# Making the gate product of a fused attention and expert kernel from half-precision parts that a DMA transposes, with the planner's table of numbers chosen anew

## The chip, the cores and the metric

The kernel runs on one core of one Trainium2 chip. The metric is device time in microseconds (us), the median of three runs. The engines are TensorE (PE in the profile, with its weight loads as PEld), VectorE (DVE), ScalarE (ACT), GpSimd (POOL), and SyncE (SP), which issues nearly all DMAs.

## The reference, cut to what matters

Three stages follow each other on 1536 tokens of width 512 (2 sequences of 768 tokens, 8 heads of 64):

```python
x   = attention(q, k, v)                 # causal window of 128, 4 sink positions
h   = x @ w_in                           # 512 -> 2048
g   = (a0 + a1*h + a2*h**2 + a3*h**3) / (1 + |b0|*|h| + |b1|*h**2 + 1e-6)
y   = g @ w_out                          # 2048 -> 512
logits = y @ w_gate                      # 8 experts
e   = argmax(logits);  p = softmax(logits)[e]
out = p * (relu(y @ w1[e]) @ w2[e])      # first `capacity` tokens of each expert, else 0
```

The kernel uses (g @ w_out) @ w_gate = g @ (w_out @ w_gate). The small matrix w_out @ w_gate, 2048 x 8, called `wgo`, gives every token's logits without its y. It is the "gate product" of this study.

## The kernel before, in words

**Work.** Attention is done in 24 halves (12 blocks of 128 tokens, two groups of heads each). The product x @ w_in with its rational function is done in 24 units (6 chunks of 256 tokens, 4 column groups of w_in); a unit is four blocks of 12 matmuls (`unit_mm`, L828), so there are 96 blocks. Float32 weights are held as the sum of two float16 tiles, a high part and a low part, and a product is three float16 passes. `conv` splits the 16 pieces of w_in and then of w_out: a load of 512 KB to a staging slot `st`, three integer operations on DVE (L315, L325, L329), the high part on ACT (L337), the low part on POOL, DVE, or ACT with PE, by a letter of the strings CI and CO (G: POOL; S: POOL; V: DVE; P and R: two opening matmuls L285, a subtracting matmul L279, ACT).

**The gate product.** `wg_group(f)` runs after each of the 16 pieces of w_out (`conv_wout` calls it). Before the change it transposes the piece on PE (L878: four 128 x 128 parts, high and low, against a float16 identity `id16`, summed in a PSUM bank), copies the bank to a float32 tile `wt` on ACT (L882), multiplies it by the float32 `wgate` on PE (L890, four column groups), copies 128 x 128 out on ACT (L892), sums the four groups on PE against a selector `gsel` (L897), and copies 128 x 8 to `wgo` on DVE (L900). `wg_split` makes the float16 parts of `wgo` for each quarter.

**What follows from it.** `first_logits` (L1092) needs all of wgo, the first tokens' g and its split; then `route` and `pick` choose the first expert on the chip, whose weights are then loaded over the tiles of w_out (`load_expert`), while PE makes y (`ffn_y`, L1110 and L1130), the expert's hidden layer and the outputs (`outp`, L1154). The units of the later chunks are worked off in between, until the end.

**What sets the order.** Every job is a Python generator that names, before each step, the engine, an assumed duration and the slots that it takes (`yield PE(0.45, "b", "wt")`). The class `Plan` walks through the jobs, gives each engine the ready step that can start first, with ties by a key, and writes the instructions in that order. Engines run their own instructions in order. The keys, letters and slot counts come from the table PRM; PRM is what "the order" means here. Where PE would stand idle by the planner's reckoning in the first part of the program, the planner writes filler matmuls of 256 columns (`idle`, L491). A step on SP counts as done `lat` plus 2.1 us after its issue:

```python
AFTER = {"PE": 0.2, "ACT": 0.17, "DVE": 0.16, "POOL": 0.12, "SP": 2.1}
```

The slots that matter: `b` (PSUM banks), `st` (2 staging tiles), `wf` (512-column scratch tiles), `wt` (1).

Of the kernel before, what the change touches and what calls it, by code (L numbers as in the profile page):

```python
# [19 lines left out]
P = 128  # L20
# [15 lines left out]
CH = 256  # L36
NCH = NT // CH
NU = 4 * NCH
PRM = dict(LA=11.205, RATE=1.224, LC=6.29, LO=5.079, BATCH=1, T0=-15.603, dS=1.502, TW=50.81, dW=6.982,
           T1=-24.174, d1=6.704, T2=67.865, d2=5.437, CI='PSPPSGGGGGGGVPPG', CO='GGGSVGPRVSSSSGGG',  # L40
           RE='PPPPPSSPPPSPPSSSPPPPPPPP', CC='G', LL=3, rb=5, gp=5, GS='GVVGGGGV', VE=1, rr=13.375, rs=42.651,
           rt=-30.248, LD=-7.643, TF=150, FG=0.033, NE=6, eps=0, WT=-60.91, NB=4, VS1=14, BK=-26.717, dK=13.517,
           dO=0.808, eb=2, SE='G', st=2, wf=2, rc=1, xt=2, ab=2, qb=2)


class Plan:
# [147 lines left out]
def SP(dur, *take, lat=0.0):  # L194
    return "SP", dur, take, lat, None, None
# [10 lines left out]
def _build(ctx, tc, nc, io, ns, window, cap):  # L206
# [21 lines left out]
    def wf_(k):  # L228
        return stg.tile([P, 512], I32, name=f"wf{k}")
# [13 lines left out]
    def bank(k):  # L243
        return (bps[0] if k < R["NB"] else bps[1]).tile([P, 512], F32, name=f"b{k}")
# [8 lines left out]
            plan.give(slot, tok)  # L253

    for name, n in (("st", R["st"]), ("wf", R["wf"]), ("g", R["gp"]), ("rb", R["rb"]), ("rc", R["rc"]), ("xt", R["xt"]),
                    ("e", R["eb"]), ("a", R["ab"]), ("mx", 4), ("q", R["qb"]), ("k", 3), ("v", 3), ("wt", 1), ("sc", 1),
                    ("b", R["NB"])):
        plan.slot(name, range(n))

# [1 line left out]
    ident = cst.tile([P, P], F32, name="ident")  # L261
    lmask = cst.tile([P, 4, P], U8, name="lmask")
    ones16 = cst.tile([P, P], F16, name="ones16")
    id16 = cst.tile([P, P], F16, name="id16")
    n16 = [cst.tile([P, P], F16, name=f"n16{j}") for j in range(2)]
    tri16 = cst.tile([P, P], F16, name="tri16")
    gsel = cst.tile([P, E], F32, name="gsel")
# [186 lines left out]
    qp = pool(att, "qp", 1)  # L454
    ahp = pool(att, "ahp", 1)
    kp = pool(att, "kp", 1)
    wgt = pool(att, "wgt", 1)
    ps_s = None if dense else pool(ctx, "ps_s", 1, space=PSUM)
    vs = [kp.tile([96, DM], F16, name=f"vs{b}") for b in range(B)] if ns else None
    smask = [kp.tile([P, 4, ns], F32, name=f"smk{i}") for i in range(2)] if ns else None  # L460
# [408 lines left out]
    def wg_group(f):  # L869

        yield ("wait", "wgate")
        yield ("wait", "c3")
        yield PE(0.45, "b", "wt", cols=512)
        kb = plan.got("b")
        tp = bank(kb)
        for d in range(KD):
            for j in range(2):
                T.matmul(out=tp[:, d * P:(d + 1) * P], lhsT=w_out[j][:, f, d * P:(d + 1) * P], rhs=id16,  # L878
                         start=(j == 0), stop=(j == 1))
        yield ACT(0.478)  # L880
        wt = wgt.tile([P, KD, P], F32, name="wt")
        A.activation(out=wt, in_=tp.rearrange("p (d f) -> p d f", d=KD), func=AF.Copy, scale=2.0 ** -8)  # L882
        plan.give("b", kb)
        yield PE(0.36, "b", cols=166)
        kb = plan.got("b")
        wp = bank(kb)

        wg = wgate.rearrange("p k e -> p (k e)")
        for d in range(KD):
            T.matmul(out=wp[32 * d:32 * d + 32, 0:P], lhsT=wg, rhs=wt[:, d, :], start=True, stop=True)  # L890
        yield ACT(0.16)
        A.activation(out=wt[:, 0, :], in_=wp[:, 0:P], func=AF.Copy)  # L892
        plan.give("b", kb)
        yield PE(0.14, "b", cols=40)
        kb = plan.got("b")
        wp = bank(kb)
        T.matmul(out=wp[:, 0:E], lhsT=wt[:, 0, :], rhs=gsel, start=True, stop=True)  # L897
        plan.give("wt", 0)
        yield DVE(0.07)
        V.tensor_copy(out=wgo[:, f, :], in_=wp[:, 0:E])  # L900
        plan.give("b", kb)
# [449 lines left out]
    def gate_weights():  # L1351
        yield SP(0.6)
        SY.dma_start(out=wgate, in_=io["wg"].rearrange("(k p) e -> p k e", p=P))

    def identities16():
        yield ("wait", "ident")
        yield ACT(0.5)
        A.activation(out=n16[0], in_=ident, func=AF.Copy, scale=-2.0 ** -8)
        A.activation(out=n16[1], in_=ident, func=AF.Copy, scale=-2.0 ** 8)
        A.activation(out=id16, in_=ident, func=AF.Copy)  # L1360

    def constants3():
        yield ("wait", "ident")
# [258 lines left out]
```

## Time and profile before

| | |
|---|---|
| median of 3 runs | 343.35 us (342.74 to 344.38) |
| the profiled execution's own time | 343.65 us |
| its span, first to last instruction | 342.0 us |
| PE busy | 322.9 us (94%) |
| DVE busy | 263.5 us (77%) |
| ACT busy | 243.8 us (71%) |
| POOL busy | 196.3 us (57%) |
| mean granted TensorE clock | 0.989 |

A busy share is a mean over stages with different limits. Matmuls are pipelined, so the "mean ns" of one matmul is a latency; what it takes of PE is read from the starts of two blocks that follow each other. The profiled execution stands 0.3 us above the median of the runs.

### The profile page before, as it was taken

The numbers are of one execution on the slowest core, as the hardware profiler recorded it, in microseconds if no ns is written. First come the engines' busy times: TensorE is split into PE (matmuls) and PEld (weight loads), VectorE is DVE, ScalarE is ACT, GpSimd is POOL, SyncE is SP. The second block draws the span as 40 slices with busy tenths as digits, with TensorE's granted clock in tenths as the row PEclk, the third lists the DMA queues.
The fourth block names the chain that finished last, engine by engine and source line by source line (L and its number), as shares of the span: only waits on it lengthen the run. The fifth ranks groups of instructions, "written<-read, shape, count | busy, mean of one in ns | idle before, by whom it ended". The sixth has DMA issues, their size and how long they took to land.

```text
span 342.0 us, 9047 instructions
## 1 busy us (share of the span) xinstructions
PE 322.9 (94%) x3605; PEld 240.1 (70%) x3605; DVE 263.5 (77%) x509; ACT 243.8 (71%) x604; POOL 196.3 (57%) x209
## 2 busy tenths in 40 slices
PE   7999999988999999999999987999999999999990
PEld 5657787666786888788878876566667678777540
DVE  5988799999999987999997887740028898786641
ACT  2798889989989999899998954351038567586610
POOL 5467869496798658798998773310040054466400
PEclk9999999999999999999999998999999999999997
DMA  7755854846366490045211200300002431000001
GB/s 227 255 188 186 246 191 136 272 143 195 126 214 217 138 357 35 2 164 178 73 39 50 94 2 2 124 2 0 2 0 72 173 127 63 0 2 0 33 32 39
DMA packets 15336, 37.59 MB, mean 110 GB/s; under 512 B 2424, under 2 KB 2424, under 8 KB 15288
## 3 DMA queue, kind: packets, MB, share of 16 engines
q1 hardware_dynamic: 15288, 36.96, 32.4%
q8 instruction: 30, 0.49, 0.6%
q14 instruction: 18, 0.15, 0.1%
HBM read 30.66 MB, written 6.29 MB: 108 GB/s over the span
## 4 chain that ended last, share of the span: by engine, by line
PE 70%; ACT 12%; DVE 11%; DMA 3%; issue 2%; SPq 0%; POOL 0%; ACTq 0%; DVEq 0%
PE b L828 25%; PE b L1110 9%; PE b L1154 5%; PE b L491 4%; PE b L1130 4%; PE b L766 4%; PE sc L650 4%; PE b L926 3%; PE b L708 2%; ACT e L680 2%; PE b L1092 2%; ACT g L834 2%; PE b L878 2%; DMA st<-w_in 1%; DVE b L325 1%
## 5 line engine op out<-in xcount | busy, mean ns | idle before, releaser
L828 PE MATMUL b<-xt,win 128*128 128x256 f16 x1152 | 138.1, 273 | 1.6 <-POOL win L355 0.6
L828 PEld LDWEIGHTS <-win 128*128 128x128 f16 x1152 | 110.6, 99 | 22.5 <-issue 8.1
L853 POOL TENSOR_TENSOR rb<-rb,rc 128x1024 f32<-128x1024 f32 x24 | 58.7, 2446 | 1.0
L850 POOL TENSOR_SCALAR rc<-rb,cof 128x1024 f32<-128x1024 f32 x24 | 30.0, 1251 | 39.7 <-ACT rb L832 39.5
L700 POOL TENSOR_TENSOR e<-e,rs 128x512 f32<-128x512 f32 x24 | 25.3, 1052 | 38.7 <-DVE rs L687 20.6
L832 ACT ACTIVATE rb<-b 128x512 f32<-128x512 f32 x48 | 29.2, 608 | 19.0 <-PE b L828 18.6
L836 DVE TENSOR_TENSOR g<-g,b 128x512 f32<-128x512 f32 x48 | 32.7, 682 | 11.5 <-ACT g L834 11.3
L834 ACT ACTIVATE g<-b,cof 128x512 f32<-128x512 f32 x48 | 37.7, 785 | 0.0
L838 DVE SCALAR_TENSOR_TENSOR g<-g,cof,b 128x512 f32<-128x512 f32 x48 | 35.7, 743 | 0.8
L680 ACT ACTIVATE e<-sc,nm 128x132 f32<-128x132 f32 x84 | 31.5, 375 | 1.9
L1110 PE MATMUL b<-gs,wout 128*128 128x384 f16 x192 | 32.5, 326 | 0.0
L735 POOL TENSOR_SCALAR_AFFINE_SELECT upp<-low 128x512 f32<-128x512 f32 x20 | 14.1, 706 | 30.7 <-ACT low L729 30.7
L856 ACT ACTIVATE rb<-rb 128x1024 f32<-128x1024 f32 x24 | 25.4, 1057 | 7.6 <-POOL rb L853 7.6
L1110 PEld LDWEIGHTS <-wout 128*128 128x128 f16 x192 | 18.5, 99 | 13.1 <-issue 1.6
L1432 DVE SCALAR_TENSOR_TENSOR g<-g,cof,b 128x512 f32<-128x512 f32 x36 | 26.0, 743 | 1.2 <-ACT b L1420 0.9
L491 PE MATMUL b<-const-bfloat16-1.0 128*1 128x256 bf16 x162 | 23.2, 283 | 2.9 <-PEq L1611 0.9
L1420 ACT ACTIVATE b<-rb 128x512 f32<-128x512 f32 x36 | 21.4, 610 | 1.5 <-DVE wgo L900 1.4
L650 PE MATMUL sc<-kt,qt 64*64 64x128 f32 (+4 forms) x672 | 19.8, 249 | 0.9 <-DMA kt<-k 0.9
L650 PEld LDWEIGHTS sc<-kt,qt 64*64 64x64 f32 x672 | 17.0, 132 | 4.8 <-issue 2.3
L491 PEld LDWEIGHTS <-const-bfloat16-1.0 128*1 128x1 bf16 x162 | 12.4, 86 | 11.2 <-issue 6.2
L1114 DVE SCALAR_TENSOR_TENSOR gse<-b,gse 128x384 f16<-128x384 f32 x4 | 2.2, 558 | 22.5 <-ACT gse L1112 22.5
L766 PE MATMUL b<-low,v 128*64 128x128 f32 x192 | 18.9, 279 | 0.0
(187 smaller groups left out, 649.6 us busy)
## 6 DMA issues: line engine op xcount, KB each, us to landing
st<-w_in SPq DMA_DIRECT2D x16, 512.0 KB, 4.2
st<-w_out SPq DMA_DIRECT2D x16, 512.0 KB, 3.4
st<-w SPq DMA_DIRECT2D x8, 512.0 KB, 3.8
kt<-k SPq DMA_DIRECT2D x12, 264.0 KB, 4.1
qt<-q SPq DMA_DIRECT2D x12, 256.0 KB, 3.9
v<-v SPq DMA_DIRECT2D x12, 256.0 KB, 3.0
xs<-xt SPq DMA_DIRECT2D x12, 256.0 KB, 4.2
out<-wf SPq DMA_DIRECT2D x12, 256.0 KB, 4.3
```

The costliest lines, as they stand in the source:

```text
L491: T.matmul(out=fp[0:1, 0:256], lhsT=one[:, 0:1], rhs=one, start=True, stop=True)
L650: T.matmul(out=out, lhsT=q[:, t], rhs=kk[:, a:z], start=True, stop=True)
L680: A.activation(out=e[:, h, :], in_=wv[:, h, :], func=AF.Exp, scale=0.125, bias=nm[:, h:h + 1], accum_out=su[:, h:h + 1])
L766: T.matmul(out=o[r, c], lhsT=v_t[jobs[j][1]][:, hd], rhs=jobs[j][0][:, 2 * par + c, :], start=st, stop=sp, skip_group_check=c > 0)
L828: T.matmul(out=out, lhsT=l, rhs=r, start=(j == 0), stop=(j == len(jobs) - 1))
L832: A.activation(out=bb, in_=hp, func=AF.Abs, scale=2.0 ** -16)
L834: A.activation(out=g, in_=hp, func=AF.Identity, scale=cof[:, 3:4], bias=cof[:, 2:3])
L836: V.tensor_tensor(out=g, in0=g, in1=hp, op=ALU.mult)
L838: V.scalar_tensor_tensor(out=g, in0=g, scalar=cof[:, 1:2], in1=hp, op0=ALU.add, op1=ALU.mult)
L850: (G if eng == "G" else V).tensor_scalar(out=cc, in0=bb, scalar1=cof[:, 5:6], scalar2=cof[:, 4:5], op0=ALU.mult, op1=ALU.add)
L853: G.tensor_tensor(out=bb, in0=bb, in1=cc, op=ALU.mult)
L1110: T.matmul(out=yp[:, :n], lhsT=l, rhs=r, start=(j == 0), stop=(j == len(jobs) - 1))
```

## The change

The piece of w_out is no longer transposed on PE. SP issues two DMA transposes for each piece (L877 of the changed kernel), from the high and the low tile of w_out to one `wf` scratch tile, 128 x 512 float16 each. `wgate` is split once into two float16 tiles `gate16`. The product is three float16 passes over four column groups, 12 matmuls (L885). The copy of the transposed piece on ACT and the slot `wt` are gone, and `id16` is made only in the part of the program that runs when tokens are left over.

```diff
-        yield PE(0.45, "b", "wt", cols=512)
-        kb = plan.got("b")
-        tp = bank(kb)
-        for d in range(KD):
-            for j in range(2):
-                T.matmul(out=tp[:, d * P:(d + 1) * P], lhsT=w_out[j][:, f, d * P:(d + 1) * P], rhs=id16,
-                         start=(j == 0), stop=(j == 1))
-        yield ACT(0.478)
-        wt = wgt.tile([P, KD, P], F32, name="wt")
-        A.activation(out=wt, in_=tp.rearrange("p (d f) -> p d f", d=KD), func=AF.Copy, scale=2.0 ** -8)
-        plan.give("b", kb)
-        yield PE(0.36, "b", cols=166)
+        yield SP(1.2, "wf", lat=1.2)
+        kw = plan.got("wf")
+        w = wf_(kw)
+        wt = [w.bitcast(F16)[:, j * 512:(j + 1) * 512].rearrange("p (d f) -> p d f", d=KD) for j in range(2)]
+        for j in range(2):
+            SY.dma_start(out=wt[j], in_=w_out[j][:, f, :], transpose=True)
+        yield PE(0.3, "b", cols=400)
         kb = plan.got("b")
         wp = bank(kb)
-        wg = wgate.rearrange("p k e -> p (k e)")
-        for d in range(KD):
-            T.matmul(out=wp[32 * d:32 * d + 32, 0:P], lhsT=wg, rhs=wt[:, d, :], start=True, stop=True)
+        g = [t.rearrange("p k e -> p (k e)") for t in gate16]
+        for j, (a, b_) in enumerate(((g[0], wt[0]), (g[0], wt[1]), (g[1], wt[0]))):
+            for d in range(KD):
+                T.matmul(out=wp[32 * d:32 * d + 32, 0:P], lhsT=a, rhs=b_[:, d, :], start=(j == 0), stop=(j == 2))
         yield ACT(0.16)
-        A.activation(out=wt[:, 0, :], in_=wp[:, 0:P], func=AF.Copy)
+        wq = w.bitcast(F32)[:, 0:P]
+        A.activation(out=wq, in_=wp[:, 0:P], func=AF.Copy, scale=2.0 ** -16)
...
+        yield ACT(0.1)
+        A.activation(out=gate16[0], in_=wgate, func=AF.Copy, scale=256.0)
+        yield DVL(0.1)
+        V.scalar_tensor_tensor(out=gate16[1], in0=wgate, scalar=256.0, in1=gate16[0], op0=ALU.mult, op1=ALU.subtract)
```

In PRM nearly every key is another number. The letters that change: two pieces of w_out go from G to P (CO ends in GPP, before GGG), four splits of g that DVE made are made by POOL (GS is all G), some units' reciprocals change their path (RE), there are three `wf` slots in place of two, and the conversions of w_out get keys that lie closer together:

```diff
-PRM = dict(LA=11.205, RATE=1.224, LC=6.29, LO=5.079, BATCH=1, T0=-15.603, dS=1.502, TW=50.81, dW=6.982,
+PRM = dict(LA=11.877, RATE=1.2, LC=6.882, LO=2.195, BATCH=1, T0=-13.679, dS=1.29, TW=53.523, dW=7.072,
...
-           dO=0.808, eb=2, SE='G', st=2, wf=2, rc=1, xt=2, ab=2, qb=2)
+           dO=0.252, eb=2, SE='G', st=2, wf=3, rc=1, xt=2, ab=2, qb=2)
```

First place, PE around one gate product, the program before. Tiles carry a number that rises in the order in which the planner wrote the program; `b_` is a PSUM bank, `xt` the transposed x, `win` a part of w_in. The transposing matmuls stand four times as shown.

```order
L828 MATMUL b_1827<-xt_896,win_97 128x256
L878 LDWEIGHTS wout_98
L878 MATMUL b_1849<-id_87,wout_98 128x128
L878 LDWEIGHTS wout_99
L878 MATMUL b_1849<-id_87,wout_99 128x128
...
L828 MATMUL b_1827<-xt_897,win_96 128x256
...
L890 MATMUL b_1881<-wt,wgate 32x128 x4
```

The same place after the change. The product reads `wf_1806`, the scratch tile that the second pair of DMA transposes fills; between the writing of that tile and its reading PE has a filler, four transposes with their fifth (L707, L711) and one block of 12 (L827, bank 1883).

```order
L827 MATMUL b_1730<-xt_895,win_98 128x256
L490 MATMUL b_1866<-const-bfloat16-1.0 1x256
L707 MATMUL b_1868<-ident,e_1746 128x128 x4
L711 MATMUL b_1873<-ident,es_128 96x128
L827 MATMUL b_1883<-xt_895,win_97 128x256
...
L885 LDWEIGHTS gate_95
L885 MATMUL b_1905<-wf_1806,gate_95 32x128
...
L893 MATMUL b_1941<-gsel,wf_1806 128x8
```

The eight transposing matmuls are gone from PE, the four float32 products (L890) have become twelve float16 ones (L885), and what PE waits for is a DMA where it was a copy on ACT.

Second place, SP's queue where the loads of w_out begin, before (`st` is a staging tile, `qt`, `kt`, `v` a block of the attention's inputs):

```order
L295 DMA st_1549<-w_out 128x1024
L597 DMA v_1595<-v 128x512
L295 DMA st_1629<-w_out 128x1024
L295 DMA st_1708<-w_out 128x1024
L295 DMA st_1791<-w_out 128x1024
L586 DMA qt_1843<-q 128x512
```

And after:

```order
L295 DMA st_1595<-w_out 128x1024
L596 DMA v_1627<-v 128x512
L295 DMA st_1643<-w_out 128x1024
L877 DMA_TRANSPOSE wf_1701<-wout_99 128x4x128
L877 DMA_TRANSPOSE wf_1701<-wout_100 128x4x128
L295 DMA st_1728<-w_out 128x1024
L877 DMA_TRANSPOSE wf_1806<-wout_99 128x4x128
L877 DMA_TRANSPOSE wf_1806<-wout_100 128x4x128
L295 DMA st_1842<-w_out 128x1024
```

Each pair of transposes stands between loads of the next pieces, and a pair waits in SP's queue until the low part of its piece is written. Over the whole order the filler matmuls go from 162 to 201; of the 39 more, nearly all stand between the 11th and the 16th of the 96 blocks of `unit_mm`.

## Rows read from the trace of the kernel before

**Rows 1.** The page: span, and busy time, share and instructions of each engine.

```profile
span 342.0 us, 9047 instructions
PE 322.9 (94%) x3605; PEld 240.1 (70%) x3605; DVE 263.5 (77%) x509; ACT 243.8 (71%) x604; POOL 196.3 (57%) x209
```

**Rows 2.** Busy time by stretch: length, then each engine, granted clock, DMA share, GB/s.

```profile
60.00:84.00 24.00, 20.50 (x261) 14.97 (x258) 23.34 (x43) 21.85 (x61) 16.62 (x16) 1.00 0.64 210
84.00:110.00 26.00, 24.70 (x305) 20.23 (x305) 25.72 (x49) 23.95 (x60) 22.16 (x20) 1.00 0.54 173
110.00:202.00 92.00, 91.78 (x1217) 75.11 (x1216) 82.50 (x154) 85.18 (x218) 74.61 (x67) 1.00 0.32 109
202.00:208.00 6.00, 3.15 (x31) 2.61 (x30) 4.51 (x15) 1.27 (x2) 3.56 (x3) 1.00 0.00 0
208.00:212.00 4.00, 4.00 (x33) 3.28 (x31) 2.28 (x8) 2.25 (x5) 1.29 (x3) 0.57 0.02 4
216.00:283.00 67.00, 67.00 (x528) 43.58 (x529) 34.75 (x56) 29.07 (x60) 14.77 (x13) 1.00 0.19 66
```

**Rows 3.** Waits of PE: for whom, us in total, times, longest.

```profile
PE b L996 <- DVE run L992: 2.4, 1, 2.4
PE b L890 <- ACT wt L882: 1.2, 3, 0.6
...
PE sc L650 <- DMA kt<-k: 0.9, 1, 0.9
...
PE b L997 <- DVE run L994: 0.4, 1, 0.4
```

**Rows 4.** The lines of the gate product: instructions, ns min/median/max, first and last start.

```profile
L878 PE MATMUL b<-id,wout x128: 216/219/229, 86.6 to 186.7; 128*128 128x128 f16 x128
...
L890 PE MATMUL b<-wt,wgate x128: 272/273/298, 88.4 to 188.4; 128*32 128x128 f32 x128
...
L882 ACT ACTIVATE wt<-b x16: 578/598/701, 87.6 to 187.1; 128x512 f32<-128x512 f32 x16
```

**Rows 5.** PE in order of time around two gate products: start, us, instructions merged.

```profile
125.47 0.43 PE L890 MATMUL b<-wt,wgate 128*32 128x128 f32 x8
125.82 0.28 PE L279 MATMUL b<-xt,n 128*128 128x256 f16 x1
...
129.25 0.61 PE L878 MATMUL b<-id,wout 128*128 128x128 f16 x8
129.69 0.49 PE L828 MATMUL b<-xt,win 128*128 128x256 f16 x3
```

**Rows 6.** PE in order of time where two short float16 passes stand.

```profile
92.14 0.25 PE L764 MATMUL b<-sh,vs 96*64 96x128 f16 x2
92.22 0.39 PE L766 MATMUL b<-low,v 128*64 128x128 f32 x4
```

**Rows 7.** PE in order of time around a conversion of the path P or R.

```profile
110.32 0.38 PE L285 MATMUL b<-const-bfloat16-1.0 128*128 128x256 bf16 x2
110.54 0.34 PE L897 MATMUL b<-gsel,wt 128*128 128x8 f32 x2
...
115.14 0.39 PE L279 MATMUL b<-wout,n 128*128 128x512 f16 x1
115.36 0.38 PE L828 MATMUL b<-xt,win 128*128 128x256 f16 x2
```

**Rows 8.** DMA issues, 84 to 190 us: count, KB each, median us to landing.

```profile
st<-w_out SPq DMA_DIRECT2D x13, 512.0 KB, 3.4
out<-wf SPq DMA_DIRECT2D x9, 256.0 KB, 4.4
...
v<-v SPq DMA_DIRECT2D x4, 256.0 KB, 3.4
```

**Rows 9.** The slowest DMA issues of the first 10 us.

```profile
wgate<-wg SPq DMA_DIRECT2D x1, 16.0 KB, 3.7
prm<-a SPq DMA_DIRECT2D x1, 2.0 KB, 5.9
```

**Rows 10.** A stretch of the chain that ended last: fillers on PE.

```profile
8.17 5.09 PE b L491 x45
```

**Rows 11.** DVE's and POOL's instructions at the routing, in order of time.

```profile
203.36 2.34 POOL L853 TENSOR_TENSOR rb<-rb,rc 128x1024 f32<-128x1024 f32 x1
...
203.43 2.32 DVE L961 TENSOR_TENSOR fi<-lg,fm 128x32 f32<-128x32 f32 x1
```

More of the change, by code (lines that the diff above doesn't have):

```diff
@@ L38 @@
 NU = 4 * NCH
-PRM = dict(LA=11.205, RATE=1.224, LC=6.29, LO=5.079, BATCH=1, T0=-15.603, dS=1.502, TW=50.81, dW=6.982,
-           T1=-24.174, d1=6.704, T2=67.865, d2=5.437, CI='PSPPSGGGGGGGVPPG', CO='GGGSVGPRVSSSSGGG',
-           RE='PPPPPSSPPPSPPSSSPPPPPPPP', CC='G', LL=3, rb=5, gp=5, GS='GVVGGGGV', VE=1, rr=13.375, rs=42.651,
-           rt=-30.248, LD=-7.643, TF=150, FG=0.033, NE=6, eps=0, WT=-60.91, NB=4, VS1=14, BK=-26.717, dK=13.517,
-           dO=0.808, eb=2, SE='G', st=2, wf=2, rc=1, xt=2, ab=2, qb=2)
+PRM = dict(LA=11.877, RATE=1.2, LC=6.882, LO=2.195, BATCH=1, T0=-13.679, dS=1.29, TW=53.523, dW=7.072,
+           T1=-22.973, d1=6.206, T2=67.305, d2=5.26, CI='PSPPSGGGGGGGVPPG', CO='GGGSVGPRVSSSSGPP',
+           RE='PPPPSPPPPPSPPSSSPPPPPPSS', CC='G', LL=3, rb=5, gp=5, GS='GGGGGGGG', VE=1, rr=19.539, rs=36.318,
+           rt=-29.499, LD=-6.009, TF=150, FG=0.033, NE=7, eps=0, WT=-60.39, NB=4, VS1=14, BK=-29.251, dK=12.297,
+           dO=0.252, eb=2, SE='G', st=2, wf=3, rc=1, xt=2, ab=2, qb=2)
 class Plan:
@@ L255, in _build @@
     for name, n in (("st", R["st"]), ("wf", R["wf"]), ("g", R["gp"]), ("rb", R["rb"]), ("rc", R["rc"]), ("xt", R["xt"]),
-                    ("e", R["eb"]), ("a", R["ab"]), ("mx", 4), ("q", R["qb"]), ("k", 3), ("v", 3), ("wt", 1), ("sc", 1),
+                    ("e", R["eb"]), ("a", R["ab"]), ("mx", 4), ("q", R["qb"]), ("k", 3), ("v", 3), ("sc", 1),
                     ("b", R["NB"])):
@@ L263, in _build @@
     ones16 = cst.tile([P, P], F16, name="ones16")
-    id16 = cst.tile([P, P], F16, name="id16")
     n16 = [cst.tile([P, P], F16, name=f"n16{j}") for j in range(2)]
@@ L271, in _build @@
     wgate = cst.tile([P, KD, E], F32, name="wgate")
+    gate16 = [cst.tile([P, KD, E], F16, name=f"gate16{j}") for j in range(2)]
     w_in = [wts.tile([P, KD, FF], F16, name=f"win{j}") for j in range(2)]
@@ L456, in _build @@
     kp = pool(att, "kp", 1)
-    wgt = pool(att, "wgt", 1)
     ps_s = None if dense else pool(ctx, "ps_s", 1, space=PSUM)
@@ L896, in wg_group @@
         wp = bank(kb)
-        T.matmul(out=wp[:, 0:E], lhsT=wt[:, 0, :], rhs=gsel, start=True, stop=True)
-        plan.give("wt", 0)
+        T.matmul(out=wp[:, 0:E], lhsT=wq, rhs=gsel, start=True, stop=True)
+        plan.give("wf", kw)
         yield DVE(0.07)
@@ L1275, in rows @@
     def rows():
+        id16 = gx.tile([P, P], F16, name="id16")
+        V.tensor_copy(out=id16, in_=ident)
         for c in range(NCH):
@@ L1359, in identities16 @@
         A.activation(out=n16[1], in_=ident, func=AF.Copy, scale=-2.0 ** 8)
-        A.activation(out=id16, in_=ident, func=AF.Copy)
     def constants3():
```

## The prediction

> **What bounds the kernel now.** I read the page first: PE is busy for 94% of the span, DVE for 77%, ACT for 71% [rows 1]. A mean does not say where PE is the limit, so the busy time by stretch comes next [rows 2]. From 60 to 84 us PE is not the limit: it is busy 20.5 of 24 us with fillers in it, and DVE 23.3 of 24. From 84 to 110 us both are full, PE 24.7 and DVE 25.7 of 26 us. From 110 to 202 us PE alone is full, 91.8 of 92 us, with DVE at 90%. Then comes the routing: PE is busy 3.2 of 6 us, and in the 4 us after that its granted clock is 0.57, so it ran mostly at the lower of its two levels. From 216 to 283 us PE is full again. All 16 gate products lie between 86.6 and 188.4 us [rows 4], that is in the stretches where PE has next to nothing free. The view of PE's waits confirms it: the longest is the routing's 2.4 us, then come 1.2 us in which the product L890 waited for ACT's copy, and for a DMA it waited just once, 0.9 us [rows 3].
>
> So what the change takes from PE should be seen in the end time, and so should everything that makes PE wait.
>
> **What it removes.** A transposing block of eight matmuls (L878) takes 0.44 us of PE, from its start to the next block's, 129.25 to 129.69 [rows 5]; it is 128 instructions, 16 such blocks [rows 4]: 16 x 0.44 = 7.0 us. Its 219 ns per matmul are a latency and do not enter. A float32 product (L890) takes 0.35 us, 125.47 to 125.82 [rows 5], 16 of them 5.6 us. PE's waits for the copy on ACT go with the copy: 1.2 us [rows 3]. Together 13.8 us. ACT loses 16 copies of 0.6 us, 9.6 us [rows 4]; ACT is full nowhere from 110 us on (85 of 92 us), so I count nothing for it beyond the waits.
>
> **What it adds on PE.** Twelve float16 passes of 128 columns, each with its own load of 32 weight columns. No row shows this. The float32 block has eight records in 0.35 us, 44 ns each; two float16 passes in 64 columns took 0.08 us, 40 ns each [rows 5, 6]. With 40 ns the block takes 0.48 us, 7.7 us for 16. The bounds: the float32 pass lasts 273 ns where the float16 one lasts 219 [rows 4], so its columns hold the array about 54 ns longer, which is twice as long; if the columns set the 44 ns, a float16 pass takes 22, the block 0.27 and the sixteen 4.2 us. If it takes what a transposing matmul takes, 0.44/8 = 55 ns, they come to 10.6 us. I stay at 40 ns because four column groups alternate in the new block as two do in [rows 6].
>
> Two pieces of w_out go from POOL to the path with PE: per piece two opening matmuls, 0.22 us, and one subtracting matmul of 512 columns, 0.22 us [rows 7]; two pieces make 0.9 us.
>
> **What it adds in waits.** PE now waits for a DMA before each product. The pair of transposes moves 256 KB in two issues. Copies of 256 KB landed 3.4 to 4.4 us after their issue in the stretch where the products lie [rows 8]. The order is made so that PE reaches the product when the planner takes the pair for landed, which by the code is 1.2 + 1.2 + 2.1 = 4.5 us after SP starts it; the order rows show it for `wf_1806`, with a filler, five transposes and a block between. If a pair lands like these copies it is there in time, on the mean by 0.6 us. The spread eats some of that: I put 0.06 us per product, 1.0 us in all. Below it is nothing. Above, a pair could take 5.9 us like the slowest small copy [rows 9], late by 1.4 us, 22 us in all.
>
> A pair also stands in SP's queue until POOL or ACT has written the low part, and the loads of the next pieces and of q, k and v stand behind it. A load takes 3.4 us for 512 KB [rows 8], and two staging slots let one piece be loaded while the other is split; PE's one wait for a load of 0.9 us says that loads come early now. I count nothing. If that cover goes, a late k makes the first matmuls of a half wait, and then DVE's maximum behind them.
>
> **What the order moves.** The two splits of 1024 columns and two of 512 go from DVE to POOL, which has 4 us free of 26 before 110 us [rows 2]. The order has 39 fillers more, at 5.09/45 = 0.113 us each [rows 10] 4.4 us, before the 16th block, where DVE is the limit: conversions of w_out start a little earlier there. What DVE is spared and what it gets earlier stand against each other, and I enter nothing, with 4.4 us as a bound on the side of a loss and 3 us, about the splits' DVE time in a full stretch, on the side of a gain.
>
> **The sum.** -7.0 - 5.6 - 1.2 + 7.7 + 0.9 + 1.0 = -4.2 us. The profiled execution took 343.65 us, 0.3 us above the median of 343.35 us; from the median this is 339.2 us, 1.2% faster. About 0.5%, 1.7 us, is what a measurement of this kernel can tell from no change. With the passes' bounds alone (4.2 to 10.6 us) it would be 335.7 to 342.1 us.
>
> **A page against it.** The Trainium skill, "VectorE: DVE Perf Modes", section "The three transpose paths", gives 1309 ns for a 128 x 128 transpose by DMA and 390 ns on TensorE, and its rules say to use TensorE where PSUM will do as destination. Eight such tiles one after the other make, as an estimate from that page, 10.5 us for a pair, 6 us later than the order expects, and 16 x 6 = 96 us in all. No run here shows a DMA transpose yet. "Advanced Engine Details and Errata", section "X-Bar Transpose (TRN2)", says instead that they are as fast as ordinary DMAs, by which my sum stands.
>
> **The rivals.**
>
> *Late pairs (slower).* Each pair lands later than PE arrives, PE stops in front of L885, and everything behind it in PE's queue stops too. For it: nothing in the trace shows this kind of DMA, and PE has no slack from 84 us on. Against it: 4.5 us were left where copies of that size take 3.4 to 4.4. A mean lateness of (4.2 + 1.0)/16 = 0.33 us uses the gain up, 0.43 us makes the kernel slower by 0.5%. At 0.7 us it gives 339.2 - 1.0 + 11.2 = 349.4 us. Chance 0.18.
>
> *Pieces in series (much slower).* The two transposes of a pair land one after the other, each no faster than a 16 KB copy, 3.7 us [rows 9]: 7.4 us, late by 2.9, 16 x 2.9 = 46 us, 384 us. Chance 0.05. The page's 1309 ns would give it by another way.
>
> *The freed time is not used (no change).* Up to 110 us DVE is full too, and five products lie there. If nothing comes of these, 5 x (0.44 + 0.35 - 0.48) = 1.6 us and the 1.2 us of waits are lost from the gain, and some 1.5 of the 4.4 us of fillers turn out to be real idle time: 339.2 + 4.3 = 343.5 us. For it: DVE at 25.7 of 26 us. Against it: from 110 us on PE alone is full, and 11 products lie there. Chance 0.17.
>
> *The routing's hole closes (faster still).* Before, PE stood 2.4 and 0.4 us in the routing [rows 3] and then ran 4 us at a granted clock of 0.57 [rows 2], 1.7 us lost. DVE's comparison L961 took 2.32 us, side by side with POOL's multiplication L853 of 2.34 us [rows 11]. If the new order parts the two, up to 4.5 us are won: 334.7 us. Against it: the new order has the same single block between the logits and the matmul that waits. Chance 0.11.
>
> **How the numbers follow.** The forecast as above has 0.49, with 335.7 to 341.6 us as its own range. Faster by over 0.5% is below 341.6 us: the forecast and the closed hole, 0.49 + 0.11 = 0.60. Within 0.5% is the third rival, 0.17. Slower is 0.18 + 0.05 = 0.23. The range from 334 to 347 us takes in the closed hole, the unused time, and of the late pairs those up to 0.55 us late; left out are most of the late pairs and the pieces in series, just under 0.2.
>
> **What would show it.** Right: the PE block L885 about 0.5 us from start to start; L877 to landing under 4.5 us; the waits of PE for `wf` from a DMA about 1 us in sum; the stretch from 110 us to the routing full on PE and shorter. Wrong: L885 at the head of PE's waits with a DMA as releaser, half a microsecond or more each; a k or w_out load that PE or DVE waits for where a pair stands before it in SP's queue; DVE full and PE waiting up to 110 us with the routing no earlier; or L885 well above 0.67 us a block.

## The result, and the profile after

The changed kernel takes 341.46 us (median of 13 runs), the kernel before, run beside it, 344.1 us: a ratio of 0.9913, 95% interval 0.989 to 0.9936. That is 0.9% faster, 3.0 us (2.2 to 3.8). The forecast was 339.2 us with a range of 334 to 347. The page of the changed kernel, to be read against [rows 1]:

```profile
span 340.8 us, 9053 instructions
PE 321.9 (94%) x3586; PEld 237.7 (70%) x3586; DVE 258.8 (76%) x505; ACT 236.6 (69%) x587; POOL 199.7 (59%) x211
...
DMA packets 32744, 41.79 MB, mean 123 GB/s; under 512 B 19832, under 2 KB 19832, under 8 KB 32696
```

PE is busy for almost as long as before. How much of that is filler stands in the groups by line, first of the kernel before, then of the changed one (busy us and mean ns behind the first bar, idle time ahead of them behind the second):

```profile
L491 PE MATMUL b<-const-bfloat16-1.0 128*1 128x256 bf16 x162 | 23.2, 283 | 2.9 <-PEq L1611 0.9 <-DVE g L838 0.9 <-ACT xt L786 0.8
```

```profile
L490 PE MATMUL b<-const-bfloat16-1.0 128*1 128x256 bf16 x201 | 29.5, 291 | 1.8 <-PEq L1612 0.9 <-ACT xt L785 0.8
```

Without fillers PE worked 322.9 - 23.2 = 299.7 us before and 321.9 - 29.5 = 292.4 us after. So 7.3 us of work are gone, and 6.3 us of fillers have come: the span fell by 1.2 us only. (This execution took 342.4 us, one of the longer ones.) The fillers did not come where the work went: 38 of the 39 more stand from 60 to 84 us, ahead of the first product, as their rows before and after show (length, busy us of the fillers and their count, clock, DMA share, GB/s).

```profile
60.00:84.00 24.00, 3.35 (x23) 1.00 0.64 210
```

```profile
60.00:84.00 24.00, 7.88 (x61) 1.00 0.57 182
```

By stretch, as in [rows 2]:

```profile
60.00:84.00 24.00, 22.52 (x254) 16.49 (x255) 22.61 (x42) 20.76 (x57) 17.55 (x17) 1.00 0.57 182
84.00:110.00 26.00, 25.23 (x372) 21.09 (x369) 24.41 (x47) 24.13 (x63) 23.02 (x23) 1.00 0.80 200
110.00:202.00 92.00, 85.08 (x1121) 67.42 (x1119) 83.19 (x169) 75.71 (x199) 73.29 (x65) 0.98 0.61 154
196.00:202.00 6.00, 3.42 (x18) 2.40 (x18) 5.26 (x18) 1.90 (x7) 1.84 (x1) 0.65 0.04 11
202.00:208.00 6.00, 6.00 (x68) 4.86 (x67) 2.08 (x13) 3.98 (x8) 1.33 (x3) 0.78 0.00 0
...
216.00:283.00 67.00, 67.00 (x550) 45.82 (x549) 33.29 (x50) 29.00 (x56) 15.72 (x14) 1.00 0.16 56
```

From 110 us on PE is no longer full (85.1 of 92 us; some 3 us of the gap are the routing's hole, which now lies at 195 to 198 us, where it was behind 202 us). The DMA share there has gone from 0.32 to 0.61, and from 0.54 to 0.80 ahead of it. PE's waits, as in [rows 3]:

```profile
PE b L992 <- DVE run L988: 2.7, 1, 2.7
...
PE b L885 <- DMA wf<-wout: 1.4, 1, 1.4
PE b L285 <- DVE g L1433: 1.0, 1, 1.0
```

The waits for the copy on ACT are gone, a wait for a pair has come, and the routing's hole has stayed. There DVE's comparison again stands beside a multiplication on POOL, as in [rows 11]:

```profile
195.83 2.06 DVE L961 TENSOR_TENSOR oh<-fx,iom 128x32 f32<-128x32 f32 x1
```

```profile
195.51 2.33 POOL L852 TENSOR_TENSOR rb<-rb,rc 128x1024 f32<-128x1024 f32 x1
```

The new lines, first the product, then the transposes (ns min/median/max, first and last start in us), and a product in PE's order of time:

```profile
L885 PE MATMUL b<-wf,gate x192: 216/219/231, 94.4 to 184.1; 128*32 128x128 f16 x192
```

```profile
L877 SPq DMA_TRANSPOSE wf<-wout x32: 1188/1224/1368, 86.2 to 179.2; - x32
...
DMA to landing us min/median/max: 2.4/3.5/6.7
```

```profile
100.26 0.35 PE L885 MATMUL b<-wf,gate 128*32 128x128 f16 x12
100.55 1.27 PE L827 MATMUL b<-xt,win 128*128 128x256 f16 x10
```

Twelve passes take 0.29 us from start to start (0.48 was forecast). A transpose of 128 KB lands 3.5 us after its issue (median), like the copies of [rows 8], which are two to four times as large; but its issue keeps SP busy for 1.22 us. A pair takes some 2.5 us of SP, where the planner books 1.2 us (`SP(1.2, "wf", lat=1.2)`). The place of the one wait, on SP:

```profile
114.10 2.51 SPq L877 DMA_TRANSPOSE wf<-wout  x2
116.71 2.12 SPq L295 DMA_DIRECT2D st<-w_out  x2
118.88 5.20 SPq L877 DMA_TRANSPOSE wf<-wout  x4
124.18 0.53 SPq L585 DMA_DIRECT2D qt<-q  x1
```

From 114 to 124 us SP spends 7.7 us on issues of transposes, and the second part of a pair landed 6.7 us after its issue, at 126.87 us.

### The profile page after: what moved, and what is told of

The parts are those of the page before. It is cut to its first block, busy times and chain, and to the rows that moved or that the text cites. A ratio compares the mean times of both kernels' runs of the same rounds, so it can differ in the third digit from the quotient of the medians.

```text
span 340.8 us, 9053 instructions
## 1 busy us (share of the span) xinstructions
PE 321.9 (94%) x3586; PEld 237.7 (70%) x3586; DVE 258.8 (76%) x505; ACT 236.6 (69%) x587; POOL 199.7 (59%) x211
## 3 DMA queue, kind: packets, MB, share of 16 engines
q1 hardware_dynamic: 32696, 41.15, 41.6%
## 4 chain that ended last, share of the span: by engine, by line
PE 75%; DVE 14%; ACT 4%; DMA 3%; issue 2%; DVEq 0%; ACTq 0%
PE b L827 29%; PE b L1106 9%; PE b L490 7%; PE b L1150 5%; PE b L1126 5%; PE b L765 4%; PE sc L649 4%; PE b L707 3%; PE b L922 3%; DMA wf<-wout 2%; DVE b L315 2%; DVE g L1433 1%; PE b L279 1%; DMA st<-w_out 1%; PE b L763 1%
## 5 line engine op out<-in xcount | busy, mean ns | idle before, releaser
L827 PE MATMUL b<-xt,win 128*128 128x256 f16 x1152 | 139.6, 276 | 0.3
L827 PEld LDWEIGHTS <-win 128*128 128x128 f16 x1152 | 112.1, 100 | 21.1 <-issue 5.7
L852 POOL TENSOR_TENSOR rb<-rb,rc 128x1024 f32<-128x1024 f32 x24 | 57.5, 2396 | 1.4
L849 POOL TENSOR_SCALAR rc<-rb,cof 128x1024 f32<-128x1024 f32 x24 | 28.9, 1202 | 20.0 <-ACT rb L831 19.7
L833 ACT ACTIVATE g<-b,cof 128x512 f32<-128x512 f32 x48 | 37.5, 784 | 0.0
L837 DVE SCALAR_TENSOR_TENSOR g<-g,cof,b 128x512 f32<-128x512 f32 x48 | 35.5, 742 | 0.7
L490 PE MATMUL b<-const-bfloat16-1.0 128*1 128x256 bf16 x201 | 29.5, 291 | 1.8 <-PEq L1612 0.9
L490 PEld LDWEIGHTS <-const-bfloat16-1.0 128*1 128x1 bf16 x201 | 16.0, 88 | 12.4 <-issue 6.2
L1433 DVE SCALAR_TENSOR_TENSOR g<-g,cof,b 128x512 f32<-128x512 f32 x34 | 24.3, 742 | 0.5
L1421 ACT ACTIVATE b<-rb 128x512 f32<-128x512 f32 x34 | 20.3, 611 | 0.5 <-DVE wgo L896 0.4
L366 POOL TENSOR_TENSOR gs<-g,gs 128x1024 f16<-128x1024 f32 (+1 forms) x8 | 13.2, 1649 | 10.5 <-ACT gs L363 10.5
L1108 ACT ACTIVATE gse<-b 128x384 f16<-128x384 f32 x4 | 2.0, 491 | 24.9 <-PE b L1106 24.9
```

The costliest lines, as they stand in the source:

```text
L490: T.matmul(out=fp[0:1, 0:256], lhsT=one[:, 0:1], rhs=one, start=True, stop=True)
L827: T.matmul(out=out, lhsT=l, rhs=r, start=(j == 0), stop=(j == len(jobs) - 1))
L833: A.activation(out=g, in_=hp, func=AF.Identity, scale=cof[:, 3:4], bias=cof[:, 2:3])
L837: V.scalar_tensor_tensor(out=g, in0=g, scalar=cof[:, 1:2], in1=hp, op0=ALU.add, op1=ALU.mult)
L849: (G if eng == "G" else V).tensor_scalar(out=cc, in0=bb, scalar1=cof[:, 5:6], scalar2=cof[:, 4:5], op0=ALU.mult, op1=ALU.add)
L852: G.tensor_tensor(out=bb, in0=bb, in1=cc, op=ALU.mult)
```

## The experiments

Each ran beside the kernel before; the ratios are to it, with 95% intervals. Against them stands the changed kernel with 0.9913 (0.989 to 0.9936). By these intervals the difference of two such ratios is itself uncertain by some 0.35 to 0.7 points, 1.2 to 2.4 us (an estimate); where a difference is given with a range below, it is by the ratios.

**Code and order apart (e1, e2).** e1 is the changed code with the table PRM of before, as in the diff; e2 the code of before with the new table.

```
-PRM = dict(LA=11.877, RATE=1.2, LC=6.882, LO=2.195, BATCH=1, T0=-13.679, dS=1.29, TW=53.523, dW=7.072,
...
-           dO=0.252, eb=2, SE='G', st=2, wf=3, rc=1, xt=2, ab=2, qb=2)
+PRM = dict(LA=11.205, RATE=1.224, LC=6.29, LO=5.079, BATCH=1, T0=-15.603, dS=1.502, TW=50.81, dW=6.982,
...
+           dO=0.808, eb=2, SE='G', st=2, wf=2, rc=1, xt=2, ab=2, qb=2)
```

> The changed code with the table of numbers of the kernel before (two slots wf). Theory A (the code gives the gain, and the order only decides how much of it is kept): PE's work falls by about the same 8 us, an order not chosen for this code makes PE wait for more pairs and frees less, so 340 to 344 us. Theory B (the new order gives the gain, the new code next to nothing): no gain, 344 us or above.

> The code of the kernel before with the new table of numbers. Theory A: the order alone brings nothing, and since it is not chosen for the longer product it loses, 344 to 349 us. Theory B: 341 to 342 us, as fast as the changed kernel.

e1: 362.98 us, ratio 1.0554 (1.0522 to 1.0587). e2: 343.31 us, ratio 0.9992 (0.9973 to 1.0011). Theory B falls by e2: the order alone brings nothing. A was right on that, but the loss that it expected for e2 did not come, and it was too mild on e1: the code in an order not chosen for it loses 18.8 us. Between 190 and 210 us of e1 DVE is the one full engine and PE waits at the lower clock:

```profile
190.00:200.00 10.00, 4.38 (x55) 3.37 (x55) 9.84 (x16) 7.00 (x20) 6.41 (x8) 0.59 0.38 114
200.00:210.00 10.00, 5.61 (x89) 3.85 (x89) 9.32 (x15) 5.06 (x15) 8.90 (x9) 0.56 0.31 71
```

DVE is still converting pieces there (L315 to L329), and the first logits on PE start at 229.2 us (193.0 us in the changed kernel). What delays the conversions no run takes apart. At equal numbers, e2 against the changed kernel, the code is worth 0.8 points, some 2.7 us (1.7 to 3.7), though e2 has no hole at the routing (its longest wait there is 0.4 us) and the changed kernel has one of 2.7 us.

**What PE's time at the product is worth (e3).**

```
-        for j, (a, b_) in enumerate(((g[0], wt[0]), (g[0], wt[1]), (g[1], wt[0]))):
+        for j, (a, b_) in enumerate(2 * ((g[0], wt[0]), (g[0], wt[1]), (g[1], wt[0]))):
             for d in range(KD):
-                T.matmul(out=wp[32 * d:32 * d + 32, 0:P], lhsT=a, rhs=b_[:, d, :], start=(j == 0), stop=(j == 2))
+                T.matmul(out=wp[32 * d:32 * d + 32, 0:P], lhsT=a, rhs=b_[:, d, :], start=(j == 0), stop=(j == 5))
...
-        A.activation(out=wq, in_=wp[:, 0:P], func=AF.Copy, scale=2.0 ** -16)
+        A.activation(out=wq, in_=wp[:, 0:P], func=AF.Copy, scale=2.0 ** -17)
```

> The changed kernel with each of the twelve passes of L885 done twice (the copy halves the sum, so the output stays), every other instruction in the same order. Theory A (PE's time at the products is on the path): a block goes from 0.28 to 0.56 us, 16 x 0.28 = 4.5 us longer, 345.9 us. Theory C (time freed on PE at the products is mostly not used, since DVE or a transfer sets the pace there): under 2 us longer, below 343.4 us.

342.92 us, ratio 0.9965 (0.9939 to 0.9991): 1.5 us more by the medians (0.6 to 3.0). Both numbers in the expectation rest on a doubled block of 0.56 us. It takes 0.45 us, as PE's order of time shows:

```profile
99.99 0.52 PE L885 MATMUL b<-wf,gate 128*32 128x128 f16 x24
100.44 1.48 PE L827 MATMUL b<-xt,win 128*128 128x256 f16 x12
```

The second dozen costs 0.16 us, so 16 x 0.16 = 2.6 us of PE were added, and 1.5 us arrived at the end; the first logits came 1.3 us later. That is between A and C by the medians, and the range does not exclude that all of it arrives. Besides, PE waits for no pair in e3's profile: seven blocks stand ahead of the changed kernel's one wait of 1.4 us, so some 7 x 0.16 = 1.1 us of what was added went into that wait (an estimate), which leaves 1.5 us. So e3 does not show that DVE or a load takes what PE has free.

**Without the wait for the pair (e4).**

```
-        for j, (a, b_) in enumerate(((g[0], wt[0]), (g[0], wt[1]), (g[1], wt[0]))):
+        for j, (a, b_) in enumerate(((g[0], w_out[0]), (g[0], w_out[1]), (g[1], w_out[0]))):
             for d in range(KD):
-                T.matmul(out=wp[32 * d:32 * d + 32, 0:P], lhsT=a, rhs=b_[:, d, :], start=(j == 0), stop=(j == 2))
+                T.matmul(out=wp[32 * d:32 * d + 32, 0:P], lhsT=a, rhs=b_[:, f, d * P:(d + 1) * P], start=(j == 0), stop=(j == 2))
...
-        wq = w.bitcast(F32)[:, 0:P]
+        wq = cst.tile([P, P], F32, name="wq")
```

> The changed kernel, in which L885 reads w_out itself instead of the transposed pair, and L888 writes a tile of its own; the transposes are still done in the same places. The gate product is then another one, so the routing sorts the tokens otherwise. Theory A (the wait for a pair costs what PE shows, 1.4 us at one place): 339.5 to 340.3 us. Theory D (a late pair costs more than that, since it also pushes what DVE and ACT do next): 338 us or less. Theory C: no change, 341 to 342 us.

339.06 us, ratio 0.9864 (0.9837 to 0.9892): 2.4 us less by the medians (0.5 to 2.9), and the first logits 1.6 us earlier, at 191.4. Theory C falls, if narrowly. The medians lie between A's 1.4 us and D's 3.5, but A's 1.4 us is well inside the range: that the wait costs more than PE's own row has is not shown. What comes behind the routing is not the same work in e4, since the tokens are sorted otherwise; the first logits stand ahead of it.

**The fillers (e5).**

```
+                nf.append(0)
+                if 136 <= len(nf) <= 196:
+                    continue
                 T.matmul(out=fp[0:1, 0:256], lhsT=one[:, 0:1], rhs=one, start=True, stop=True)
```

> The changed kernel without the 61 fillers that PE executes between 60 and 84 us; every other instruction in the same order. At 84 us the changed kernel has done 51.5 us of PE work other than fillers, the kernel before 54.7 us. Theory A (those 3.2 us are idle time that the new order has because DVE and ACT set the pace there, and fillers only stand in it): 341 to 342 us, or some longer if PE's clock falls in the gaps. Theory E (the fillers themselves hold up the matmuls behind them): 3 to 4 us less, 337.5 to 338.5 us.

340.38 us, ratio 0.99 (0.9866 to 0.9933): no difference that the intervals show. Without them PE's granted clock falls to 0.58 and 0.57 in the two stretches from 72 to 80 us, after one of 4 us with PE busy for 0.84; at 84 us as much is done either way (194 matmuls of `unit_mm`, 193 with fillers). The fillers stand in idle time; theory E falls. A gain that the lower clock uses up would not show here.

**The hole at the routing (e6).**

```
-        G.tensor_tensor(out=bb, in0=bb, in1=cc, op=ALU.mult)
+        for z in (slice(0, 512), slice(512, 1024)):
+            G.tensor_tensor(out=bb[:, z], in0=bb[:, z], in1=cc[:, z], op=ALU.mult)
```

> The changed kernel with each of POOL's 24 multiplications L852 of 1024 columns done as two of 512, so that none lasts 2.3 us; every other instruction in the same order. Theory A (DVE's comparison L961 in the routing takes 2.06 us because POOL's 2.33 us run beside it, and PE's longest wait of 2.7 us and the low clock behind it follow from that): the wait falls to about 1.5 us and the kernel to 339.5 to 340.5 us. Theory F (the place of the comparison in the order makes the hole, whatever POOL does): 341 to 342 us.

341.68 us, ratio 0.9912 (0.9883 to 0.994): nothing won, and PE's wait is 2.6 us. The rows show why the experiment failed without deciding between A and F. DVE's and then POOL's order of time: the comparison (L962) now stands beside the first half and the cast behind it (L982) beside the second.

```profile
195.16 0.98 DVE L962 TENSOR_TENSOR oh<-fx,iom 128x32 f32<-128x32 f32 x1
196.17 1.18 DVE L982 CAST oh<-oh 128x32 f16<-128x32 f32 x1
```

```profile
194.84 2.48 POOL L853 TENSOR_TENSOR rb<-rb,rc 128x512 f32<-128x512 f32 x2
```

**The zeros (e7).**

```
             yield from pick()
+            for i in range(NST // P, NBLK):
+                SY.dma_start(out=io["out"][i * P:(i + 1) * P, :].rearrange("p (a c) -> p a c", c=P),
+                             in_=zt.unsqueeze(1).to_broadcast([P, DM // P, P]))
...
+    zt = cst.tile([P, P], F32, name="zt")
...
             yield SP(0.73)
-            SY.dma_start(out=io["out"][i * P:(i + 1) * P, :], in_=zt)
```

> The changed kernel with the nine DMAs that write zeros to the output, 2.4 MB between 115 and 125 us, issued after the routing instead (from a zero tile of their own); every other instruction in the same order. Theory G (the late pair at 126.9 us is late because it shares the DMA engines with these nine): PE's wait for a pair of 1.4 us goes, 339 to 340 us, near the 339.1 us of the run without the wait. Theory H (it is late because four transposes follow each other in SP's queue): the wait stays, 341 to 342 us.

342.29 us, ratio 0.9939 (0.9905 to 0.9974): not better. The premise of G was wrong: in the changed kernel the nine DMAs leave SP between 126.3 and 131.6 us, not between 115 and 125, and the late part, issued at 120.18 us, landed at 126.87 us.

```profile
L1383 SPq DMA_DIRECT2D out<-wf x9: 383/656/1308, 126.3 to 131.6; - x9
```

So they can't be what made it late but for its last 0.6 us. In e7's profile the wait at that place is gone, but PE comes to that product 3.6 us later (128.81 instead of 125.25 us), held up by another wait ahead of it; the 0.5 us that are left belong to a later pair. PE's waits, and the place in the chain that ended last:

```profile
PE b L285 <- DVE g L1436: 2.6, 1, 2.6
...
PE b L885 <- DMA wf<-wout: 0.5, 1, 0.5
```

```profile
107.52 0.57 DVE g L837
108.09 5.58 DMA st<-w_out
113.67 0.03 issue
```

A load of w_out landed 5.58 us after its issue, DVE stood 3.1 us for it, PE 2.6 us for DVE, and PE's clock fell to 0.59 behind that. The zeros come later than this load in either kernel, so it is not their doing: the changed kernel has the load at the same place, 108.15 us, right behind a pair that took SP from 105.54 us on, and there it landed after 4.0 us. The transposes are slow at different places too: with landings of up to 6.7 us in both profiles, in the changed kernel among those issued from 118.9 to 122.9 us, in e7 among those from 110.8 to 115.6 us. What makes such a stretch is open; G is not borne out, and H is not shown.

**The price of a pair on SP (e8, e10, e9).** Three edits of the same two lines: a second pair behind each; two plain copies of the same bytes behind each; and both parts in one tile, transposed by one issue (the views that later hold an expert's weights follow that tile).

```
         for j in range(2):
             SY.dma_start(out=wt[j], in_=w_out[j][:, f, :], transpose=True)
+        for j in range(2):
+            w2 = kp.tile([P, KD, P], F16, name=f"wt2{j}")
+            SY.dma_start(out=w2, in_=w_out[j][:, f, :], transpose=True)
```

> The changed kernel with a second pair of the same transposes behind each pair, into a tile that nothing reads; every other instruction in the same order. Theory A (SP and the DMA engines have room, what a pair costs is only whether it lands in time): the second pairs take 2.4 us of SP each and delay some loads, 341.5 to 343.5 us. Theory I (the transposes weigh on the DMA side, so that loads of w_out, q, k and v come late behind them): 16 x 2.4 us more of SP's queue show as 345 us or more, with PE or DVE waiting for loads.

```
+        for j in range(2):
+            w2 = kp.tile([P, KD, P + 8], F16, name=f"wt2{j}")
+            SY.dma_start(out=w2[:, :, 0:P], in_=w_out[j][:, f, :].rearrange("p (d f) -> p d f", d=KD))
```

> The changed kernel with two plain copies of the same 128 x 512 parts, in pieces of 256 bytes, behind each pair, into tiles that nothing reads; every other instruction in the same order. It adds the bytes of the doubled pairs (which took 366.0 us) without their time on SP: a plain issue takes about 0.35 us. Theory J: 32 x 0.35 = 11 us more on SP, less than a third of the doubled pairs' 39 us: 342 to 349 us. Theory K: the traffic alone makes the pairs and loads late, 355 us or more.

```
-    w_out = [wts.tile([P, KF, DM], F16, name=f"wout{j}") for j in range(2)]
+    wo2 = wts.tile([P, KF, 2, DM], F16, name="wout")
+    w_out = [wo2[:, :, j, :] for j in range(2)]
...
-        for j in range(2):
-            SY.dma_start(out=wt[j], in_=w_out[j][:, f, :], transpose=True)
+        SY.dma_start(out=w.bitcast(F16).rearrange("p (d f) -> p d f", f=P),
+                     in_=wo2[:, f].rearrange("p j d -> p (j d)"), transpose=True)
```

> The changed kernel with both parts of w_out in one tile, so that a pair is one transpose of 128 x 1024 instead of two of 128 x 512; every other instruction in the same order. Theory J (the price of a pair is SP's time, 2 x 1.22 us, in which the loads behind it wait): if the one issue takes some 1.3 us, SP gets back 16 x 1.2 = 19 us and the kernel takes 338.5 to 340.5 us; if it takes 2.4 us, nothing is won, 341 to 342 us. Theory K (the price is what the transposes do on the DMA engines): 341 to 342 us, even with the shorter issue.

e8: 366.04 us, ratio 1.0619 (1.0574 to 1.0663). e10: 354.41 us, ratio 1.0242 (1.018 to 1.0304). e9: 338.41 us, ratio 0.9836 (0.9792 to 0.9879), clear of the changed kernel's interval. Theory A falls with e8; I's number holds there. In e8 PE waits for the pair ten times, 11.7 us in all, and DVE waits four times, 11.4 us, for loads of w_out that stand behind the pairs (0.6 us in the changed kernel). In e10 PE waits for the pair eight times, 8.5 us. SP's order of time in e8 where that is worst, a load of w_out behind four transposes, and the chain that ended last at the same place:

```profile
112.12 3.41 SPq L877 DMA_TRANSPOSE wf<-wout  x2
115.63 2.52 SPq L880 DMA_TRANSPOSE wt<-wout  x2
118.24 0.54 SPq L295 DMA_DIRECT2D st<-w_out  x1
```

```profile
118.24 3.84 DMA st<-w_out
...
122.20 0.43 DVE wf L315
```

From 114 to 124 us PE is busy 4.9 of 10 us there, DVE 2.7 and POOL not at all. The copies of e10, and the transposes of e9, on SP (ns min/median/max):

```profile
L880 SPq DMA_DIRECT2D wt<-wout x32: 593/620/1408, 87.6 to 193.4; - x32
```

```profile
L877 SPq DMA_TRANSPOSE wf<-wout x16: 1232/1238/1857, 87.2 to 176.1; - x16
...
DMA to landing us min/median/max: 3.1/4.2/5.5
```

e8 adds 32 x 1.22 = 39 us to SP and 24.6 us to the time. e10 adds 32 x 0.62 = 20 us to SP, with no fewer bytes than e8 (21.5 MB against 20.1 MB on the queue from 84 to 190 us) and more packets, and 13.0 us to the time. e9 moves the same bytes as the changed kernel with 16 x 1.24 = 20 us instead of 39 us on SP, wins 3.1 us (1.0 to 4.3), and PE waits for no pair. What the transfers took of the 16 DMA engines goes another way than the time: 41.6% of the span or 142 us in the changed kernel, 141 us in e9, 161 in e8 and 164 in e10. So the loss follows SP's time and not the bytes: J. J's number for e10 failed all the same, 354.4 us against 349 at most and close to K's 355: a copy's issue took 0.62 us, not 0.35, and only with that does half of e8's time on SP go with half of its loss. That part is fitted afterwards; e9 is the test that J passed, since an issue of double size takes as long as one of single size. What the loads gain in e9 shows in SP's order of time around the place of e7's slow load:

```profile
103.80 1.24 SPq L877 DMA_TRANSPOSE wf<-wout  x1
105.14 0.60 SPq L296 DMA_DIRECT2D st<-w_out  x1
...
108.45 0.33 SPq L296 DMA_DIRECT2D st<-w_out  x1
```

The load goes out at 105.14 instead of 108.15 us, and DVE is busy for 4.00 us of 108 to 112 us, where it has 2.81 in the changed kernel. (There the load landed at 112.15 us; the profile puts DVE's wait of 1.6 us down to ACT's L833, which ended 0.2 us later, so the load is not its only cause.) PE is nearly full again: 39.2 and 39.3 of 40 us from 110 to 150 and from 150 to 190 us, where the changed kernel has 37.4 and 38.8. The traffic is not free either: the median load of w_out landed after 4.0 us in the changed kernel and 3.9 in e9, after 3.4 before [rows 8].

**Both causes taken away (e11), and the passes again (e12).** Both start from e9; e12 adds the edit of e3, e11 these lines:

```
         yield POOL(2.34)
+        if routed:
+            G.tensor_copy(out=routed.pop(), in_=run[:, FB, 0:1])
         G.tensor_tensor(out=bb, in0=bb, in1=cc, op=ALU.mult)
...
         places(bs, bank(kb))
+        routed.append(cst.tile([P, 1], F16, name="hold"))
```

> The run with one issue per pair (338.41 us) with one tiny copy on POOL ahead of the multiplication that stood beside the routing's comparison: the copy reads what the routing writes last on DVE, so that this one multiplication starts only then; every other instruction in the same order. Theory A: comparison and cast fall from 2.06 and 0.18 us to 0.2 us each, PE's wait from 2.7 to about 0.8 us, and the low clock behind it mostly goes: 335.5 to 337 us. Theory F (the wait is set by the place of the comparison in the order): 338 to 339 us.

> The run with one issue per pair (338.41 us) with each of the twelve passes done twice, every other instruction in the same order. With two issues per pair 4.5 us more of PE cost 1.5 us. Theory J (there the loads and pairs behind SP's queue took what PE had free, and with one issue PE alone is the limit from 110 us on): close to the 4.5 us, 341.5 to 343 us. Theory C (DVE takes what PE has free in any case): below 340.5 us.

e11: 336.61 us, ratio 0.9741 (0.9694 to 0.9788), the fastest version. POOL's multiplication now starts behind the routing's last addition, comparison and cast take 0.19 and 0.18 us, and PE's wait is 0.8 us. DVE's and POOL's order of time:

```profile
192.46 0.19 DVE L966 TENSOR_TENSOR oh<-fx,iom 128x32 f32<-128x32 f32 x1
192.68 0.18 DVE L986 CAST oh<-oh 128x32 f16<-128x32 f32 x1
...
194.19 2.07 DVE L1002 TENSOR_SCALAR keep<-keep 128x4 f32<-128x4 f32 x1
```

```profile
193.88 2.35 POOL L857 TENSOR_TENSOR rb<-rb,rc 128x1024 f32<-128x1024 f32 x1
```

The 2 us have moved to L1002, where PE waits for nothing. The clock stays at 1.00 from 195 to 200 us, where e9 has 0.66. So the hole came from the multiplication beside the comparison, as A said; in e2, where POOL has nothing beside it, the comparison takes 0.19 us too. PE also waits for a pair once, 0.7 us. The gain of e11 on e9 is 1.8 us by the medians and one point by the ratios (1.1 to 5.5 us).

e12: 340.41 us, ratio 0.984 (0.9788 to 0.9892). By the medians it is 2.0 us over e9, by the ratios 0.1 us, since the kernel before took 345.8 us beside e12 and 344.2 beside e9. The time leaves this open. In the profiles, one of each, the first logits start at 191.5 instead of 189.8 us: of the 2.6 us that were added, 1.7 arrive. J's number was wrong, by the same mis-sized block as in e3 at the least; the median is inside C's bound of 340.5 us, so e12 does not show that PE alone is the limit.

## Why the prediction was right, and where its steps were off

**The sum.** -4.2 us were forecast, -3.0 us (2.2 to 3.8) came. That the number held is in part luck, since errors in both directions stood against each other. In the two profiles 7.3 us of work left PE and the span fell by 1.2 us, so 6.1 us more of PE's time went to fillers or stood idle: 3.2 us more ahead of 84 us, 3.3 us more from 84 to 190 us, 0.4 us less after that. The forecast had nothing for the first (the order), -1.2 + 1.0 us for the second (the waits), and the passes 3.1 us too dear, which made up for half of it.

**What it removes and what the passes cost.** The work taken from PE is right: with the measured block the forecast's terms make -7.0 - 5.6 + 16 x 0.29 + 0.9 = -7.1 us, and PE lost 7.3 us of work. The passes were mis-sized: 40 ns were taken from [rows 5, 6], the block shows 24, near the lower bound of 22, 4.6 instead of 7.7 us in all. e3 shows that 24 is itself a mixture: a second dozen costs 0.16 us, some 13 ns a pass, so some 0.13 us of a block come once, however many passes it has. A price per pass from another block was the wrong measure.

**"PE alone is full."** The prediction read 91.8 of 92 us in [rows 2] as a limit, so that every microsecond off PE would be one off the end. How far this held is not settled. In the changed kernel PE is idle for 3.8 of the 80 us from 110 to 190 us, where it was for 0.2 us before, so part of what was freed there went into waits; in e9's profile, with half of SP's issue time gone, 1.5 us are left. Whether DVE takes the rest (it is busy for 90% of 110 to 202 us) is argued only: e3's 1.5 of 2.6 us can be read without it, and e12's time is open.

**Waits for the pair.** 1.0 us was entered as lateness. PE's row shows 1.4; without the wait 2.4 us are won by the medians (0.5 to 2.9), and with one issue per pair, which also helps the loads, 3.1 us (1.0 to 4.3). The rival of late pairs is thus true in kind, with 0.1 to 0.2 us per pair on the mean, below the 0.33 that would have used up the gain. What was missed is SP's time. The prediction took a pair to land 3.4 to 4.4 us after SP starts it, on the mean 0.6 us ahead of the planner's 4.5. The second part goes out 1.2 us behind the first and lands 3.5 us later, some 4.7 us after SP's start (an estimate from the medians), so nothing was to spare. It also said that loads stand behind pairs on SP and entered nothing, since two staging slots cover it. A transpose's issue takes 1.22 us of SP, a load's 0.38, and the load at 108 us goes out 3.0 us earlier when half of these issues are gone. In e8, with twice the pairs, that cover does not hold: 24.6 us.

**Pages.** The pieces in series did not happen: the median transpose landed 3.5 us after its own issue, and e9's of double size after 4.2 us, not after 7.4, nor after the 10.5 us that the prediction estimated for eight tiles in a row. The Trainium skill, "Advanced Engine Details and Errata", section "X-Bar Transpose (TRN2)", says that these are as fast as ordinary DMAs. The trace agrees for the landing: 3.5 us, copies 3.4 to 4.4 [rows 8], and at equal size and place, behind each pair from 84 to 190 us, e8's transposes land after 2.5 us and e10's copies after 2.4. It does not agree for the engine that issues them, 1.22 us against a copy's 0.62 and a load's 0.38.

**The order.** Entered as nothing, with bounds of -3 and +4.4 us. e2's time says nothing (0.9992), but two things stand against each other in it. With the new table PE has done 52.0 us of work other than fillers at 84 us with the old code, 51.5 with the new, where it had done 54.7 before: the new order is 3.2 us behind there, which the prediction had as the side of a loss. In e2 the routing's hole is gone (its longest wait there is 0.4 us), in the changed kernel it is not. So in the changed kernel the order was not nothing; that its 3.2 us arrive in full at the end is argued, not tested. e1 says that the code can't be had without an order chosen for it: with the old numbers it loses 18.8 us. The fillers did turn out to stand in idle time (e5), as the rival of the unused time has it.

**The routing's hole** stayed, as the forecast had it, and for the reason that the rival named: the comparison on DVE beside the multiplication on POOL. e11 shows it by parting the two. The rival's price of up to 4.5 us was too high by the medians: 1.8 us were won, with 0.8 us of PE's wait left.

Left open: how much of e4's and e9's gain is PE's wait and how much the loads behind the pairs; what makes some landings take 6.7 us; what holds PE when it is not full; and what e12 costs in time.

## What to carry to other kernels

Before moving work from an engine to a DMA, count the issues and their time on the engine that issues them, with everything that stands behind them in its queue: here 39 us of issues on SP went with one wait of PE for a transfer in the profile, and one issue of double size in place of two, which halves these 39 us, won 3 us of the end time. A stretch in which one engine shows 99% says nothing on how far the next one is behind; doubling one small block in place can tell it, if what is added is larger than the noise and no wait ahead of it takes it up, as one did in e3. A change of order shows its price where work is left undone: compare the work without fillers at a fixed time. A short instruction that takes ten times its usual time wants a look at what runs beside it on POOL, and a dependency that parts the two can take it off the path: here it won 1.8 us.

## What the runs showed of the hardware that was not expected

The issue of a DMA transpose keeps SP busy for 1.22 us at 128 x 512 and for 1.24 us at 128 x 1024, where a load of 512 KB takes 0.33 to 0.38 (medians before and after) and a copy of 128 KB in pieces of 256 bytes 0.62 us. Behind each pair, transposes of 128 KB land after 2.5 us (e8) and such copies after 2.4 (e10). The 32 transposes raise the packets under 512 bytes from 2424 to 19832. Twelve float16 passes over four column groups take 0.29 us, 24 of them 0.45. On DVE a comparison of 32 elements per partition that takes 0.19 us by itself (e11) lasted as long as a POOL multiplication beside it (2.06 us beside 2.33); with the multiplication cut in two, one DVE instruction went by per half (0.98 and 1.18 us). The changed kernel's 13 executions had a mean granted clock between 0.984 and 0.994, and the longer ones tend to have the lower clock: 342.5 us at 0.984, 338.8 us at 0.994, but 340.3 to 342.3 us at 0.990.
